# A two-layer attention and MLP kernel whose order comes from a planner: new DMA prices, priorities by stage, and longer runs in a weight load

## The chip, the core and the metric

The kernel runs on one core of a Trainium2 chip. The metric is the device time of one launch in microseconds (us), as the median of several runs. Before the change it was 943.03 us over three runs (942.86 to 943.37).

## What is computed

The input is 2048 tokens of 576 features. Two layers with the same weights follow each other; each is an attention block and an MLP, both with a layer norm ahead and a residual sum behind. Attention has 32 heads of 18 features, and a token sees itself and the 255 tokens before it.

```python
def _A_ref(x, wqkv, wo):            # H = 32, Dh = 18, W = 256
    qkv = (x @ wqkv) ... ; q, k, v = qkv[0], qkv[1], qkv[2]
    scores = jnp.einsum("bhqd,bhkd->bhqk", q, k) * (Dh ** -0.5)
    mask = (idx[:, None] - idx[None, :] >= 0) & (idx[:, None] - idx[None, :] < W)
    p = _softmax(jnp.where(mask[None, None], scores, -1e9), axis=-1)
    return einsum("bhqk,bhkd->bhqd", p, v) ... @ wo

def _B_ref(x, w1, b1, w2, b2):      # w1: 576 x 4608
    h = _gelu(jnp.einsum("bsd,df->bsf", _layernorm(x), w1) + b1)
    return jnp.einsum("bsf,fd->bsd", h, w2) + b2

for _ in range(2):
    x = x + _A_ref(_layernorm(x), A_wqkv, A_wo)
    x = x + _B_ref(x, B_w1, B_b1, B_w2, B_b2)
```

## The kernel before

**Chunks and stages.** The work is cut into eight chunks of 512 tokens, four for each layer. The residual stream (`x_res`) and the attention weights stay in SBUF; the MLP weights w1 and w2 are read from HBM again for each chunk. A chunk k goes through these stages, whose names are those of `PL.stage`:

- `ln`: layer norm of its four 128-token tiles, and a DMA transpose of each into `xnTa` (`ln_norm_T`, issued on L590). The first chunk transposes on TensorE.
- `q<k>.<i>`: q, k and v of tile i (`qkv`, matmuls in `two_out`, L625). VectorE casts them out of PSUM (L647, L660), and q and k are transposed by a DMA (L667).
- `ea`, `eb`: head groups 0 to 3 and 4 to 7 of the attention (`E`). Scores (L695) go to PSUM, ScalarE takes the exponential (L704), GpSimd masks the band's edges (L725), and the product with V (L742) gathers in one PSUM bank. VectorE divides by the sum (L752, L757).
- `t`: the tail (`tail`): four DMA transposes of the attention output into `attT` (L786), the out-projection (L625 again, with `wo_sb`), the residual sum (L776), and the second layer norm with its transpose into `xnTm`.
- `ga`, `gb`: first and second half of the first MLP product with gelu (`G_part`: L820 for the last 64 of 576 rows, L832 for the other 512; gelu on L835).
- `ma`, `mb`: first and second half of the second MLP product (`mm2`, L860) with its residual sum (L776, or L779 into the output tile).

Stages of several chunks are in work at once: while ScalarE is busy with the exponentials of chunk k, TensorE has the MLP products of chunks k-1 and k-2.

**The planner.** The code doesn't issue instructions as it goes; each `add` makes a task with an engine, a cost, a latency and a priority. `Plan.schedule` then simulates the engines by a list: it takes, over all engines, the ready task that can start first, and between equal start times the one with the lowest priority number (L317). The order that comes out is fixed: each engine runs its own list, and waits on semaphores where a task needs another engine's result. A price that is wrong therefore does not break anything; it puts a task too early or too late in its engine's list. `nudge` adds an amount to the priorities of a stage (L204); it is empty before. Up to 140 us of the plan, where TensorE would idle for more than 0.4 us, the planner puts filler matmuls (L533).

**DMA in the plan.** One number, `dma_free`, is the time at which the transfers so far are through (L348, L349). A DMA's latency is the larger of its stated one and what the queue gives plus 1.3 us. A transfer's `move` is its bytes over 270 GB/s (`dma`, L486); transposes state a latency of 2.5 us (4.5 in chunk 0, 4.0 for the attention output) and a move of 0.6. SyncE issues nearly all of them: weight and input loads and transposes stand in one list.

**Weight slots.** `w1_load` (L596) fills one of four slots with a block of 512 columns of w1: one load of 512 KB for the first 512 rows, and two of 32 KB for the other 64 rows. These 64 rows fill only half of the array's rows, so the kernel puts two column tiles on the two halves at once: the two loads go to partitions 0 to 63 and 64 to 127, and `rest` (L814) makes four matmuls in pairs. With `(a b f)` the load for half b takes the tiles b and b+2: two runs of 128 columns, 256 bytes each. `w2_load` (L611) reads w2 in nine pieces of 288 KB for each half.

Of the kernel before, what the change touches and what calls it, by code (L numbers as in the profile page):

```python
# [184 lines left out]
class Plan:  # L185
# [15 lines left out]
        self.fifo_last = {}  # L201

    def add(self, eng, fn, reads=(), writes=(), dma=None, ring=4, cost=0.1, lat=0.1, prio=0.0, alloc=(), fifo=None, plain=False, after=(), move=0.0, hold=False):
        prio += self.nudge.get(self.stage, 0.0)  # L204
        t = Task(idx=len(self.tasks), eng=eng, fn=fn, reads=tuple(reads), writes=tuple(writes), cost=cost, lat=lat, prio=prio,
                 dma=dma, ring=ring, alloc=tuple(alloc), handles=tuple({r for r in tuple(reads) + tuple(writes) if isinstance(r, Bank)}),
                 plain=plain, move=move, fifo=fifo, hold=hold, stage=self.stage)
        pred = set()
        for r in t.reads:
            if r in self.lw:  # L210
                pred.add(self.lw[r])
        for w in t.writes:
            pred.update(self.rd.get(w, ()))
            if w in self.lw:
                pred.add(self.lw[w])
        for w in after:
            pred.update(self.rd.get(w, ()))
        for w in t.writes:
            self.lw[w] = t
            self.rd[w] = []  # L220
        for r in t.reads:
            self.rd.setdefault(r, []).append(t)
        order = set()
        if fifo is not None:
            if fifo in self.fifo_last:
                order.add(self.fifo_last[fifo])
            self.fifo_last[fifo] = t
        order -= pred
        for p in pred:
            p.succ.append((t, True))  # L230
        for p in order:
            p.succ.append((t, False))
        t.npred = len(pred) + len(order)
        for h in t.handles:
            h.left += 1
        self.tasks.append(t)
        return t
# [15 lines left out]
    def schedule(self):  # L253
# [49 lines left out]
        dma_free = 0.0  # L303
        n = len(self.tasks)
        while len(order) < n:
            best = None
            cands = []
            for e in ENGS:
                for t in released[e]:
                    st = max(free[e], t.ready)  # L310
                    got = ()
                    if t.alloc:
                        got, when = place(t)
                        if got is None:
                            continue
                        st = max(st, when)
                    key = (round(st, 3), t.prio, t.idx)  # L317
                    if e == "pe" and st < self.feed_until or t.hold:
                        cands.append((key, t, st, got))
                    if best is None or key < best[0]:  # L320
                        best = (key, t, st, got)
            assert best is not None, "stuck"
            _, t, st, got = best
            if t.eng == "pe" and t.fifo is None and st < self.feed_until and starves(t, st, got):
                for c in sorted(cands, key=lambda c: c[0]):
                    if c[1].fifo is not None or not starves(*c[1:]):
                        _, t, st, got = c
                        break
            if t.eng == "pe" and t.fifo is None:
                for c in cands:  # L330
                    if c[1].hold and c[2] <= st + self.hold:
                        _, t, st, got = c
            if t.eng == "pe" and st < self.warm_until and st - free["pe"] > 0.4:
                self.keep_warm(free["pe"], st, bank_free, extra)
                free["pe"] = st
            released[t.eng].remove(t)
            for h, no in zip(t.alloc, got):
                h.no = no
                for b in h.banks():
                    del bank_free[b]  # L340
            free[t.eng] = st + t.cost
            if t.fifo == "pa":
                fed += 1
                backlog += sum(x.cost for x, data in t.succ if data and x.eng == "act")
            elif t.fifo == "act" and t.handles:
                backlog -= t.cost
            if t.dma is not None:
                dma_free = max(dma_free, st + t.cost) + t.move  # L348
                t.lat = max(t.lat, dma_free + 1.3 - st - t.cost)  # L349
            t.end = st + t.cost + t.lat  # L350
            for h in t.handles:
                h.left -= 1
                h.free = max(h.free, t.end)
                if h.left == 0:
                    for b in h.banks():
                        bank_free[b] = h.free
            for s, data in t.succ:
                same = s.eng == t.eng == "pe"
                s.ready = max(s.ready, st + t.cost + (t.lat if data and not same else 0.0))
                s.npred -= 1  # L360
                if s.npred == 0:
                    released[s.eng].append(s)
            order.append((st, t))
# [16 lines left out]
def build_kernel(nc, A_x, A_wqkv, A_wo, B_x, B_w1, B_b1, B_w2, B_b2, out):  # L380
# [9 lines left out]
    NFH = NF // 2  # L390
# [16 lines left out]
    S = Sched(nc)  # L407
    PL = Plan(S, 7)
    add = PL.add

    def sb(name, shape, dtype):
        return nc.alloc_sbuf_tensor(name, shape, dtype)
# [10 lines left out]
    qn = sb("qn", [P, NQN, H * 32], BF16)  # L423
# [62 lines left out]
    def dma(q, out_, in_, reads=(), writes=(), cls="w", ring=8, **kw):  # L486
        n = 2 if cls != "xr" else 4
        for s in out_.shape:
            n *= s
        add(q, lambda e: e.dma_start(out_, in_), reads=reads, writes=writes, dma=cls, ring=ring, lat=1.3, move=n / 270e3, **kw)  # L490

    n0 = CH[0][2]

# [28 lines left out]
    for i in range(NQN):  # L522
        add("pool", lambda e, i=i: e.memset(qn[:, i, :].rearrange("p (h e) -> p h e", e=32)[:, :, DH:32], 0.0),
            writes=[f"qn{i}h{h}" for h in range(2)], cost=0.5, prio=-9)
# [39 lines left out]
    def ln_norm_T(t, i, dst, dname, prio, src=None, srcres=None, dup=False, pe=False):  # L564
        s = x_res if src is None else src
        res = X(t) if srcres is None else srcres
        sl = xn_ctr[0] % NXN
# [3 lines left out]
            reads=res + [f"mv{t}", f"rstd{t}"], writes=[f"xn{sl}"], cost=0.6, prio=prio)  # L571
# [6 lines left out]
        if pe:  # L578
# [9 lines left out]
                reads=[b], writes=[f"{dname}{i}"], cost=0.75, lat=0.2, prio=prio)  # L588
            return
        add("sp", lambda e: e.dma_start_transpose(dst[:, :, i * 128:(i + 1) * 128], xn[:, sl, :]),  # L590
            reads=rd, writes=[f"{dname}{i}"], dma="t", ring=8, cost=1.3, lat=2.5, move=0.6, prio=prio)


    w1n = [0]

    def w1_load(prio, reads=()):  # L596
        B = w1n[0]
        if B >= NK * 9:
            return
        w1n[0] += 1  # L600
        sl = B % NB1
        bb = B % 9
        cols = slice(bb * 512, (bb + 1) * 512)
        dma("sp", w1_sb[:, sl, 0:2048].rearrange("p (c f) -> p c f", c=4), B_w1[0:512, cols].rearrange("(c p) f -> p c f", p=P),
            reads=reads, writes=[f"w1a{sl}"], cls="w1", cost=0.5, prio=prio)
        src = B_w1[512:576, cols].rearrange("p (a b f) -> p b a f", a=2, b=2)
        for b in range(2):
            dma("sp", w1_sb[64 * b:64 * b + 64, sl, 2048:2304].rearrange("p (a f) -> p a f", a=2), src[:, b],
                writes=[f"w1b{sl}_{b}"], cls="w1", cost=0.5, prio=prio)

    def w2_load(hf, prio, gate=False):  # L611
        for pr in range(NFH // 2):
            f0 = hf * NFH + 2 * pr
            dma("sp", w2_sb[:, 2 * pr:2 * pr + 2, :], B_w2[f0 * P:(f0 + 2) * P, :].rearrange("(w p) d -> p w d", p=P),
                reads=[f"h{2 * pr}"] if gate else [], writes=[f"w2s{pr}"], cls="w2", ring=9, cost=0.6, prio=prio)


    def two_out(lhs, rhs, reads, prio, after=(), fill=FILL):
# [17 lines left out]
    def qkv(k, i, prio0):  # L636
        l, t0, nt = CH[k]
        A = l * NT + t0 + i
        for n, w in enumerate("qkv"):
# [10 lines left out]
            else:  # L650
# [14 lines left out]
                else:  # L665
                    dst, dn = k_of(A)
                add("sp", lambda e, dst=dst, sl=sl: e.dma_start_transpose(dst, qn[:, sl, :]),  # L667
                    reads=[f"qn{sl}h0", f"qn{sl}h1"], writes=[dn], dma="t", ring=8, cost=1.3, lat=2.5 if k else 4.5, move=0.6, prio=prio)


    def units_of(k):
# [110 lines left out]
    def tail(k, prio):  # L782
        l, t0, nt = CH[k]
        rd = [f"aq{g}" for g in range(G)]
        for i in range(nt):
            add("sp", lambda e, i=i: e.dma_start_transpose(attT[:, :, i * 128:(i + 1) * 128], attq[:, i, :]),  # L786
                reads=rd + ["aqd"], writes=[f"aT{i}"], dma="t", ring=8, cost=1.3, lat=4.0, move=0.6, prio=prio - 0.1)
        for i in range(nt):
            t = t0 + i
            bs = two_out(lambda c, i=i: attT[:, c, i * 128:(i + 1) * 128], lambda c, s: wo_sb[:, c, s:s + HB],  # L790
# [8 lines left out]
    def G_part(k, hf, prio):  # L799
# [6 lines left out]
        while f < f1:  # L806
# [7 lines left out]
            def rest(e, fs=fs, sl=sl, bks=bks):  # L814

                ins = None
                for ff, bk in zip(fs, bks):
                    b = ff % 2
                    col = 2048 + (ff % 4) // 2 * 128
                    ins = e.matmul(bank(bk)[:, 0:n], w1_sb[64 * b:64 * b + 64, sl, col:col + 128], xnTm[64 * b:64 * b + 64, k % 2, 4, 0:n],  # L820
                                   start=True, stop=False, tile_position=(64 * b, 0))
                return ins
# [213 lines left out]
```

The softmax here doesn't subtract the row's maximum and nothing guards it: scores larger than these inputs give would overflow.

## Time and profile before

| | |
|---|---|
| time, median of 3 | 943.03 us |
| span of the profiled execution | 942.4 us, mean granted TensorE clock 0.993 |
| MLP products on TensorE, L860 / L832 / L820 | 312.1 / 259.5 / 45.0 us |
| qkv / out-projection, L625 | 134.3 / 43.1 us |
| P times V, L742; scores, L695 | 101.3; 65.1 us (and 12.3 for chunk 1's) |
| filler matmuls, L533 | 12.1 us, 70 of them |
| exponential / gelu on ScalarE | 346.8 / 197.5 us |
| SyncE's and ScalarE's DMA queues | 120.96 and 2.65 MB in 231,248 and 2,432 packets |
| GpSimd's DMA queue | 5.03 MB in 6,880 packets |
| packets under 512 B, of all | 158,768 of 240,663 |
| issue to landing, median: attT, xnTm, kT, qT, xnTa | 3.1, 3.5, 3.3, 3.6, 3.2 us |
| issue to landing, median: w1 512 KB, w1 32 KB, w2 288 KB, x 576 KB | 4.1, 3.8, 4.9, 5.9 us |

Busy times are unions: overlapping matmuls count once. A matmul's mean duration holds its latency, so the count times the mean is more than the busy time. PEld is the weight load ahead of each matmul and overlaps it. The granted clock is given as a share of full speed. A wait is put down to the semaphore that came last.

### The profile page before, as it was taken

How to read it: one execution, taken by the hardware profiler on the slowest of the kernel's cores; microseconds unless marked ns; L12 is line 12 of the kernel's file. 1: busy time of each engine (PE TensorE's matmuls, PEld its weight loads, DVE VectorE, ACT ScalarE, POOL GpSimd, SP SyncE). 2: the span in 40 equal slices, each digit the busy share in tenths (PEclk: the TensorE clock that was granted, in tenths of full speed). 3: DMA queues.
4: the chain of work that ended last, by engine and by line, in shares of the span. 5: the costliest groups of instructions: out<-in, count | busy, mean ns of one | idle time of the engine just before them, and what ended most of it. 6: DMA issues, size and time to landing. Idle time of an engine off the chain costs nothing. (4 is left out here: it accounts for less than half of the span.)

```text
span 942.4 us, 22728 instructions
## 1 busy us (share of the span) xinstructions
PE 906.8 (96%) x9353; PEld 563.4 (60%) x9402; DVE 312.2 (33%) x796; ACT 592.3 (63%) x717; POOL 369.5 (39%) x507
## 2 busy tenths in 40 slices
PE   8798999999999999999999999999999999999998
PEld 6456556564665657655575756647466574746556
DVE  6546312740272303732154321442015320242001
ACT  3687686677827777277833778458783587852541
POOL 3767444373612635135420454316362063620100
PEclk9799999999999999999999999999999999999999
DMA  9997639944295426945159251693709716184440
GB/s 218 149 208 131 171 93 245 185 114 130 60 222 134 137 79 132 172 112 164 51 112 244 60 163 52 142 208 88 216 3 222 163 42 199 30 228 130 149 139 26
DMA packets 240663, 130.10 MB, mean 138 GB/s; under 512 B 158768, under 2 KB 238384, under 8 KB 240560
## 3 DMA queue, kind: packets, MB, share of 16 engines
q1 hardware_dynamic: 231248, 120.96, 54.4%
q0 software_dynamic: 6880, 5.03, 2.9%
q10 hardware_dynamic: 2432, 2.65, 0.9%
q8 instruction: 75, 1.23, 0.5%
q14 instruction: 28, 0.23, 0.1%
HBM read 91.87 MB, written 2.36 MB: 100 GB/s over the span
## 5 line engine op out<-in xcount | busy, mean ns | idle before, releaser
L704 ACT ACTIVATE pT<-ps 128x1024 bf16<-128x1024 f32 (+2 forms) x384 | 346.8, 972 | 92.8 <-PE ps L695 91.5
L725 POOL TENSOR_SCALAR_AFFINE_SELECT pT<-pT 128x512 bf16<-128x512 bf16 (+1 forms) x368 | 279.0, 782 | 261.4 <-ACT pT L704 246.2
L835 ACT ACTIVATE hT<-ps,b1col 128x512 bf16<-128x512 f32 x288 | 197.5, 687 | 224.4 <-PE ps L832 223.3
L860 PE MATMUL ps<-w_sb,hT 128*128 128x288 bf16 x2304 | 312.1, 286 | 2.5 <-DVE x_res L776 1.2
L832 PE MATMUL ps<-xnTm,w_sb 128*128 128x512 bf16 x1103 | 259.5, 379 | 3.4 <-issue 1.1
L860 PEld LDWEIGHTS ps<-w_sb,hT 128*128 128x128 bf16 x2304 | 211.4, 97 | 75.0 <-issue 16.6
L776 DVE TENSOR_TENSOR x_res<-ps,x_res 128x288 f32<-128x288 f32 x160 | 71.2, 450 | 371.7 <-PE ps L860 352.9
L832 PEld LDWEIGHTS ps<-xnTm,w_sb 128*128 128x128 bf16 x1152 | 107.1, 98 | 132.1 <-issue 20.1
L625 PE MATMUL ps<-wqkv,xnTa 128*128 128x288 bf16 x960 | 134.3, 289 | 6.7 <-DVE qn L660 4.5
L742 PEld LDWEIGHTS ps<-vA,pT 128*128 128x128 bf16 x2880 | 92.9, 96 | 33.2 <-issue 14.6
L625 PEld LDWEIGHTS ps<-wqkv,xnTa 128*128 128x128 bf16 x960 | 88.8, 98 | 39.3 <-DVE qn L660 9.1
L742 PE MATMUL ps<-vA,pT 128*128 128x20 bf16 x2880 | 101.3, 172 | 4.4 <-DVE mv_all L548 2.8
L842 POOL TENSOR_TENSOR x_res<-x_res,b2bc 128x576 f32<-128x576 f32 x32 | 44.9, 1402 | 90.6 <-ACT hT L835 90.4
L695 PE MATMUL ps<-qT,kT 32*128 32x384 bf16 (+2 forms) x1216 | 65.1, 280 | 5.4 <-ACT pT L704 4.9
L660 DVE CAST qn<-ps 128x288 bf16<-128x288 f32 x120 | 54.2, 455 | 47.7 <-PE ps L625 47.4
L557 POOL TENSOR_SCALAR vtmp<-mv_all 128x1 f32<-128x1 f32 (+1 forms) x43 | 8.3, 192 | 154.9 <-DVE mv_all L548 154.2
L820 PE MATMUL ps<-xnTm,w_sb 64*128 64x512 bf16 x288 | 45.0, 381 | 2.5 <-ACT pT L704 1.2
L546 DVE BATCH_NORM_STATS2 st_all<-x_res 128x6 f32<-128x288 f32 x104 | 45.2, 449 | 4.8 <-DMA x_res<-in_A_x_dram 3.5
L625 PE MATMUL ps<-wo_sb,attT 128*128 128x288 bf16 x320 | 43.1, 286 | 3.7 <-DMA attT<-attq 3.7
L779 DVE TENSOR_TENSOR xn<-ps,x_res 128x288 bf16<-128x288 f32 x32 | 14.6, 458 | 93.4 <-PE ps L860 93.4
L695 PEld LDWEIGHTS ps<-qT,kT 32*128 32x128 bf16 x1216 | 19.5, 92 | 36.1 <-issue 17.9
L569 DVE TENSOR_SCALAR xn<-x_res,mv_all,rstd 128x576 bf16<-128x576 f32 x52 | 32.9, 636 | 24.6 <-DMA xnTm<-xn 14.9
(39 smaller groups left out, 280.5 us busy)
## 6 DMA issues: line engine op xcount, KB each, us to landing
w_sb<-in_B_w_dram SPq DMA_DIRECT2D x144, 288.0 KB, 4.9
w_sb<-in_B_w_dram SPq DMA_DIRECT2D x72, 512.0 KB, 4.1
w_sb<-in_B_w_dram SPq DMA_DIRECT2D x144, 32.0 KB, 3.8
x_res<-in_A_x_dram POOLq DMA_DIRECT2D x4, 1152.0 KB, 9.0
out_dram<-xn SPq DMA_DIRECT2D x16, 144.0 KB, 1.8
wqkv<-in_A_wqkv_dram ACTq DMA_DIRECT2D x3, 576.0 KB, 7.0
hT<-in_A_x_dram SPq DMA_DIRECT2D x2, 576.0 KB, 5.9
wo_sb<-in_A_wo_dram ACTq DMA_DIRECT2D x1, 576.0 KB, 5.0
```

Of the source, the lines that this page charges most:

```text
L546: add("dve", lambda e, i=i, s=s: e.bn_stats(st_all[:, t, i, :], s[:, t, i * HB:(i + 1) * HB]), reads=res, writes=[f"st{t}_{i}"], cost=0.43 ...
L625: ins = e.matmul(bank(bs[o])[:, 0:HB], lhs(c), rhs(c, o * HB), start=(c == 0), stop=(c == KD - 1))
L660: add("dve", lambda e, b=bs[o], dst=dst: e.tensor_copy(dst, bank(b)[:, 0:HB].rearrange("p (h d) -> p h d", d=DH)), reads=[bs[o]], writes=[ ...
L695: ins = e.matmul(two(bs[j // 2])[:, j % 2, col:col + nq * 128], k_of(T0 + so)[0][32 * j:32 * j + 32, g, :], qs[32 * j:32 * j + 32, g, qo * ...
L704: add("act", lambda e, h2=h2: e.activation(pT[:, sl, 2 * h2:2 * h2 + 2, lo:hi], two(bs[h2])[:, :, lo:hi], ACT.Exp, scale=SCALE), reads=[bs ...
L725: add("pool", lambda e, ap=ap, pat=pat, sgn=sgn, kind=kind: e.affine_select(ap, ap, pattern=pat, compare_op=(ALU.is_ge if kind == "d" else ...
L742: ins = e.matmul(bank(B_O)[:, o:o + VW], pT[:, sl, j, col + qi * 128:col + (qi + 1) * 128], vA[:, (T0 + so) % VS, 4 * g + j, :], start=(fi ...
L776: add("dve", lambda e: e.tensor_tensor(x_res[:, t, sl], bank(b)[:, 0:HB], x_res[:, t, sl], ALU.add), reads=[b], writes=[f"x{t}h{hh}"], cos ...
L820: ins = e.matmul(bank(bk)[:, 0:n], w1_sb[64 * b:64 * b + 64, sl, col:col + 128], xnTm[64 * b:64 * b + 64, k % 2, 4, 0:n], start=True, stop ...
L832: ins = e.matmul(bank(bk)[:, 0:n], w1_sb[:, sl, col:col + 128], xnTm[:, k % 2, c, 0:n], start=False, stop=(c == 3))
L835: add("act", lambda e, ff=ff, fl=fl, bk=bk: e.activation(hT[:, fl, 0:n], bank(bk)[:, 0:n], ACT.Gelu_apprx_tanh, bias=b1col[:, ff:ff + 1]), ...
L860: ins = e.matmul(bank(b)[:, 0:HB], hT[:, fl, i * 128:(i + 1) * 128], w2_sb[:, fl, hh * HB:(hh + 1) * HB], start=(fl == 0), stop=(fl == NFH ...
```

## The change

The planner gets another model of the DMA: each kind of transfer has a stated latency and a service time (`move`), and SyncE's transfers go through one serial queue. `nudge` is filled with amounts for 47 stage names, which were searched for on variations of the planner's own model. Loads of w1, w2 and the residual input get a stage name of their own (with `+`), so that they don't move with the stage that issues them. In the w1 remainder, the load for half b takes the tiles 2b and 2b+1 where all four tiles of the block are used together: one run of 256 columns, 512 bytes. The block that holds the boundary between the two halves of F (tiles 16 and 17 before it, 18 and 19 behind it) stays as it was, and `rest` takes the tiles in the matching order. The computation is the same.

```diff
     def add(...):
-        prio += self.nudge.get(self.stage, 0.0)
+        stage = self.stage + ("+" if dma in ("w1", "w2", "xr") else "")
+        prio += self.nudge.get(stage, 0.0)
 ...
             if t.dma is not None:
-                dma_free = max(dma_free, st + t.cost) + t.move
-                t.lat = max(t.lat, dma_free + 1.3 - st - t.cost)
+                done = max(dma_free, st + t.cost + t.lat) + t.move
+                dma_free = done if t.eng == "sp" else dma_free + t.move
+                t.lat = done - st - t.cost
 ...
+    PL.nudge = {"ld0+": 6.29, "q1.0": -32.21, "q1.2": 2.89, "q1.3": -2.43, "t0": 18.11, "ea1": 3.55, "eb1": 21.57, "ma0": 50.18, "q2.1": 34.5,
+                "q2.3": 41.3, "ea2": -33.88, "ma1+": -2.59, "q3.0": -17.85, "q3.1": -0.47, "q3.2": 6.73, "q3.3": -0.86, "t2": 1.88, "gb1": 14.71,
 ...
+                "ga6": -9.76, "ma6": 4.26}
 ...
-        add(q, lambda e: e.dma_start(out_, in_), reads=reads, writes=writes, dma=cls, ring=ring, lat=1.3, move=n / 270e3, **kw)
+        kw.setdefault("lat", 2.0)
+        kw.setdefault("move", n / 330e3)
+        add(q, lambda e: e.dma_start(out_, in_), reads=reads, writes=writes, dma=cls, ring=ring, **kw)
 ...  ln_norm_T
-            rd, ..., cost=1.3, lat=2.5, move=0.6, prio=prio)
+            rd, ..., cost=1.3, lat=0.6, move=0.8, prio=prio)
 ...  w1_load: large load
-            ..., cls="w1", cost=0.5, prio=prio)
+            ..., cls="w1", cost=0.55, lat=2.0, move=1.45, prio=prio)
         src = B_w1[512:576, cols].rearrange("p (a b f) -> p b a f", a=2, b=2)
+        if not straddles(bb):
+            src = B_w1[512:576, cols].rearrange("p (b a f) -> p b a f", a=2, b=2)
 ...  remainder loads
-                writes=[f"w1b{sl}_{b}"], cls="w1", cost=0.5, prio=prio)
+                writes=[f"w1b{sl}_{b}"], cls="w1", cost=0.6, lat=1.4, move=0.22 if straddles(bb) else 0.15, prio=prio)
 ...  w2_load
-                ..., cls="w2", ring=9, cost=0.6, prio=prio)
+                ..., cls="w2", ring=9, cost=0.55, lat=2.0, move=0.92, prio=prio)
 ...  qkv
-                    ..., cost=1.3, lat=2.5 if k else 4.5, move=0.6, prio=prio)
+                    ..., cost=1.3, lat=0.7, move=1.15, prio=prio)
 ...  tail
-                reads=rd + ["aqd"], ..., cost=1.3, lat=4.0, move=0.6, prio=prio - 0.1)
+                reads=rd + ["aqd"], ..., cost=1.3, lat=0.6, move=0.8, prio=prio - 0.1)
 ...  G_part, rest
-                for ff, bk in zip(fs, bks):
-                    b = ff % 2
-                    col = 2048 + (ff % 4) // 2 * 128
+                at = [(ff % 4, bk) for ff, bk in zip(fs, bks)]
+                if not straddles(fs[0] // 4):
+                    at = [at[i] for i in (0, 2, 1, 3)]
+                for n2, (i, bk) in enumerate(at):
+                    b = n2 % 2
+                    col = 2048 + (i // 2 if straddles(fs[0] // 4) else i % 2) * 128
```

## Prediction

> **What bounds the kernel now.** I read the page first, then the work by stretches of 20 us, then the waits of TensorE, then the timeline around the largest hole. The first two parts of the page say which engine counts:
>
> ```profile
> PE 906.8 (96%) x9353; PEld 563.4 (60%) x9402; DVE 312.2 (33%) x796; ACT 592.3 (63%) x717; POOL 369.5 (39%) x507
> ...
> PE   8798999999999999999999999999999999999998
> ...
> PEclk9799999999999999999999999999999999999999
> ```
>
> TensorE is busy for 906.8 of 942.4 us; 35.6 us are left. Some of those are no idle time: the mlp's first product (L832) has 1103 matmul records and 1152 weight loads, so 49 records are missing, and at about 0.21 us each they explain some 10 us. About 25 us of true idle remain, of which some 4 lie before the first and after the last matmul. The table of stretches shows where:
>
> ```profile
> 0.00:20.00 20.00, 18.16 (x145) 14.30 (x146) 10.86 (x30) 6.70 (x13) 7.39 (x23) 1.00 0.90 220
> 20.00:40.00 20.00, 14.50 (x184) 9.06 (x182) 13.10 (x41) 11.31 (x16) 11.76 (x16) 0.90 1.44 149
> 40.00:60.00 20.00, 17.15 (x219) 10.27 (x216) 10.09 (x22) 13.89 (x20) 13.74 (x20) 0.76 1.01 195
> 60.00:80.00 20.00, 18.89 (x308) 11.98 (x307) 8.07 (x21) 19.14 (x26) 14.95 (x21) 1.00 0.95 178
> 80.00:100.00 20.00, 17.57 (x243) 12.27 (x241) 17.14 (x45) 12.62 (x14) 13.23 (x21) 1.00 0.72 131
> 100.00:943.00 843.00, 820.56 (x8265) 505.53 (x8311) 252.95 (x641) 528.69 (x634) 308.45 (x408) 1.00 0.54 134
> ```
>
> After the window come its length, the busy time of PE, PEld, DVE, ACT and POOL, the granted clock, the DMA share and GB/s. The first 100 us hold 13.7 us of idle TensorE (1.84 + 5.50 + 2.85 + 1.11 + 2.43). In the next 842 us only about 22 are unbusy, of which the missing records take about 10 and the end of the run about 3.5: some 8 us, or 1%. The opening holds two more losses. In the five stretches, 0.90 and 0.76 are a clock at half speed for about 13.7 us; at half speed that costs 6.8 us of matmul time. And the planner's filler matmuls (L533, 12.1 us in all) are idle time that keeps the array running; by stretches, 7.2 us lie before 10 us, where the first inputs are still coming, and 4.9 us between 20 and 80 us.
>
> The timeline of TensorE, and that of VectorE, around the hole that precedes the slow clock:
>
> ```profile
> 32.94 0.93 PE L533 MATMUL ps<-warm 128*128 128x256 bf16 x7
> 33.92 0.29 PE L695 MATMUL ps<-qT,kT 32*128 32x256 bf16 x4
> 36.99 0.47 PE L742 MATMUL ps<-vA,pT 128*128 128x20 bf16 x12 [2.79 <-DVE mv_all L548]
> ...
> 34.77 1.18 DVE L546 BATCH_NORM_STATS2 st_all<-hT 128x6 f32<-128x288 bf16 x3 [3.54 <-DMA hT<-in_A_x_dram]
> ...
> 36.41 0.43 DVE L757 TENSOR_TENSOR attq<-ps,rinv 128x288 bf16<-128x288 f32 x1
> ```
>
> TensorE stands 2.79 us before the probabilities-times-V group. That group needs the mask of POOL, done at about 36.5, and the division on VectorE (L757), done at 36.84; the division stood behind layer norm statistics that waited 3.54 us for an input load. So the load itself holds TensorE up by only some 0.3 us. The rest is that, while exp, mask and division run, nothing else stands next in TensorE's order. That is a matter of order, which this change rewrites.
>
> For the long part, the waits of TensorE alone:
>
> ```profile
> PE ps L695 <- ACT pT L704: 7.1, 16, 1.2
> PE ps L625 <- DVE qn L660: 4.5, 8, 1.4
> PE ps L625 <- DMA attT<-attq: 3.7, 3, 1.4
> PE ps L742 <- DVE mv_all L548: 2.8, 1, 2.8
> ```
>
> The whole list sums to 28 us. No wait on a weight load is in it; the one DMA of weight is the transpose of the attention output before the out-projection, 3.7 us in three of eight chunks.
>
> **The Trainium skill.** "TensorE: Matmul & The Clock Gate", section "What's actually happening", says that the array falls to half clock after an idle window of about 3.4 us and needs a busy one to recover. The trace agrees in kind: clock 1.00 up to 35 us, 0.59 in 35 to 40 and 0.50 in 40 to 45, beginning inside the 2.79 us hole. "DMA: Bandwidth & Descriptors", section "Issuing engines are not separate DMA queues", says that all queues run on the same 16 engines. The trace agrees: while the bias load of POOL took 13.6 us to land, two transposes of SyncE issued between 25 and 45 us took 7.3 us at the median against 3.3 to 3.6 for the q and k transposes of the page. The same page, "Specifications", puts full rate at runs of 512 bytes or more; the packet records show 256-byte packets of about 18 ns and 1024-byte ones of about 46, so a short run does cost more per byte.
>
> **The change part by part.** *Shorter list of packets.* In eight of nine w1 blocks the two remainder loads read 512-byte runs instead of 256-byte ones. There are 144 such loads of 128 runs; 128 of them go to 64 runs, 8,192 packets less. Each pair of 256-byte packets took 36 ns, one of 512 should lie between 18 and 36: at most 8,192 x 18 ns over 16 engines, 9 us of DMA time in all against a DMA share of 0.54. No TensorE wait is for these loads, so I cost it at 0 us, hidden behind the matmuls that run while slots are loaded ahead. The matmuls of `rest` keep number, size and pairing of the row halves; only the order of the banks changes: 0 us.
>
> *DMA prices.* These act only through the order. From issue to landing, old price, new price and trace: attention transposes 5.3, 2.7, 3.1; layer norm transposes 3.8, 2.7, 3.2 and 3.5; q and k transposes 3.8 (5.8 in chunk 0), 3.15, 3.3 and 3.6; large w1 loads 3.7, 4.0, 4.1; w2 pairs 3.0, 3.5, 4.9; the 576 KB input loads 4.1, 4.4, 5.9. (Old: issue cost plus the stated latency, or plus size / 270 plus 1.3. New: cost plus latency plus service.) Loads move towards the trace, and transposes pass from too dear to too cheap by 0.2 to 0.8 us. Too dear meant that the planner put other work before the consumer, which costs nothing while such work is left; too cheap means that the consumer's place in TensorE's fixed order comes early. Behind it every later matmul is held. I take 0.4 us (3.1 - 2.7) as the low end of such a wait and 1.4 us, the longest that the trace shows on this transpose, as the high one, and expect three or four: +1.5 us net.
>
> *Stage priorities.* They add and remove no instruction of the computation; a priority decides only which of the ready tasks of an engine goes first. What can be won is idle time and slow clock. For the opening: the qkv of chunk 1 tile 0 goes far ahead (-32), the tail of chunk 0 and the second half of chunk 1's attention later. That puts ready matmuls into the stretch of 30 to 45 us, where TensorE was busy for 9.58 of 15 us. Bounds: 0 if the hole is only moved; 6.8 (clock) + 2.8 (hole) = 9.6 us if both go. I take the clock and 2.0 of the hole, 8.8 us[...]. For the steady part the bound is the 8 us above; I take half of the attention transposes' wait, 1.9 us, since moving qkv or mlp groups ahead of the out-projection hides it. Sum: -8.8 - 1.9 + 1.5 = -9.2, so 943.0 - 9.2 = 934 us.
>
> **The rivals.** *The hole stays, and the clock drops all the same.* The input load is still priced at 4.4 us, where the one in question took 6.8, and the bias load still has no service time in the plan. For it: both are visible in the lines above. Against: the load was responsible for 0.3 us only. Gain: some waits, 3 to 5 us, so 939. *No difference:* gains in the opening paid back by transposes that land later than planned, 943 +- 1.9. *Slower:* transposes are planned too early at each of eight tails, 8 x 1.4 = 11 us, and less cover ahead of them: 954; with only some tails and a slow clock that lasts as long as now, about 950. For it: the attention transposes took up to 5.0 us where weight loads were in flight, against 2.7 in the plan alone. Against: the new model queues transposes behind loads, so with a busy queue its price rises too.
>
> **How the numbers follow.** 934 in 50 of 100; 939 in 15; no difference in 9; slower in 26. So faster 0.65, same 0.09, slower 0.26. The low end, 921, is the whole of 9.6 plus the 8 us of the steady part and half of the fillers after 20 us and the rest of the opening's holes; the high end, 952, takes in most of the slower case.
>
> **What would show it.** Right: granted clock 1.00 in all stretches of the first 100 us, or a shorter slow one; TensorE's unbusy time there below 10 us; equal instruction counts but for the fillers (70 now); packets under 512 bytes down by about 16,384. Wrong: a slow clock of 13 us or more; waits of L625 on attT above 8 us in total; new waits on xnTm, xnTa or w_sb on TensorE. If TensorE's busy time outside the opening changes by more than 5 us at equal work, the order of its groups costs something that I have taken as nothing.

## Result and the profile after

The changed kernel takes 955.91 us (median of 4, 951.70 to 959.81) against 943.2 us before: a ratio of 1.0134, 95% interval 1.009 to 1.0177. It is slower by 12.7 us. Its four launches spread over 8 us and those of the kernel before over 1, but in later sessions of 15 to 47 launches the latter spread over 5 to 6 us as well.

The page of the kernel after, its first two parts:

```profile
PE 911.4 (96%) x9355; PEld 563.7 (59%) x9396; DVE 316.2 (33%) x796; ACT 592.3 (62%) x717; POOL 368.8 (39%) x507
...
PE   8889999999998999899999999998999899999998
...
PEclk9999999999999999999999999999999999999999
```

The work is the same; the fillers are 64 where they were 70, and 41 matmul records of L854 (L832 before) are missing, where 49 were. TensorE is unbusy for 42.4 us of 953.8, before for 35.6 of 942.4. Less the missing records at about 0.21 us, true idle went from some 25 to some 34 us. Its busy time rose by 4.6 us. The work by stretches, with the columns as before:

```profile
0.00:20.00 20.00, 18.46 (x140) 13.90 (x141) 10.50 (x29) 6.61 (x12) 7.23 (x23) 1.00 0.89 216
20.00:40.00 20.00, 16.23 (x192) 9.40 (x190) 13.28 (x42) 12.08 (x17) 12.51 (x17) 0.91 1.78 154
40.00:60.00 20.00, 16.92 (x249) 10.63 (x246) 11.19 (x26) 14.97 (x22) 14.14 (x21) 1.00 1.14 217
60.00:80.00 20.00, 17.95 (x278) 11.82 (x276) 8.28 (x21) 17.79 (x22) 15.28 (x21) 1.00 0.90 184
80.00:100.00 20.00, 18.18 (x281) 13.31 (x279) 17.45 (x45) 11.76 (x13) 13.38 (x22) 1.00 0.66 102
100.00:954.00 854.00, 823.63 (x8228) 504.60 (x8267) 255.51 (x636) 529.12 (x634) 306.24 (x406) 0.99 0.53 132
```

The opening did what the prediction hoped for, in part: one slow stretch of the clock, of 3.4 us in place of 13.7, and 12.3 us of unbusy TensorE in place of 13.7. All of the loss lies behind it: unbusy time after 100 us went from 21.8 to 30.2 us, and the clock is no longer full there. TensorE's own list of waits shows what came in:

```profile
PE ps L714 <- DMA kT<-qn: 5.4, 2, 4.0
PE ps L644 <- DMA xnTa<-xn: 5.3, 2, 2.8
PE ps L644 <- DVE qn L679: 3.2, 7, 0.8
PE ps L842 <- DMA w_sb<-in_B_w_dram: 3.2, 2, 2.6
...
PE ps L714 <- ACT pT L723: 2.4, 7, 0.8
...
PE ps L644 <- DMA attT<-attq: 2.0, 4, 1.3
...
PE ps L882 <- DMA w_sb<-in_B_w_dram: 1.8, 2, 1.4
```

Before, TensorE waited 3.9 us for transposes and never for a load of w1 or w2; after, the lines put down to the transposes of k, of the layer norm and of the attention output and to the weight loads come to 17.7 us, in a few long waits (1.4 us of it, one wait on k, lies in the opening). The search also won something: the waits on the exponential went from 7.1 to 2.4 us.

The longest of them, on TensorE and then on SyncE's queue (start, duration of the issue):

```profile
753.26 3.63 PE L854 MATMUL ps<-xnTm,w_sb 128*128 128x512 bf16 x16
760.85 0.56 PE L714 MATMUL ps<-qT,kT 32*128 32x384 bf16 x8 [3.96 <-DMA kT<-qn]
...
751.85 0.47 SPq L502 DMA_DIRECT2D w_sb<-in_B_w_dram  x1
752.41 1.23 SPq L602 DMA_TRANSPOSE xnTm<-xn  x1
753.69 2.87 SPq L686 DMA_TRANSPOSE kT<-qn  x1
756.61 1.31 SPq L686 DMA_TRANSPOSE qT<-qn  x1
```

Behind three w2 loads and a transpose, the issue of kT held SyncE for 2.87 us where 1.29 is its median. The line names kT, but kT landed at 759.90 us, 0.95 us before TensorE went on. What ended the hole is the transpose of q behind it: the scores read it, TensorE's own wait on its semaphore lasts from 756.04 to 760.80 us, and it landed at 760.76, 4.2 us after its issue at 756.61. So the held-up issue of kT cost TensorE time by making the next issue late. The same is seen at the holes that end at 295.88 and 404.62 us: there a layer norm transpose and a w1 load landed 2.6 and 3.7 us after their issue, about as usual; their issue was late.

Stretches of half clock follow three of the long holes; after the clock come the DMA share and GB/s:

```profile
290.00:295.00 5.00, 3.10 (x17) 1.47 (x15) 3.49 (x10) 3.85 (x5) 0.93 (x3) 1.00 1.01 225
295.00:300.00 5.00, 4.12 (x26) 2.32 (x27) 3.25 (x7) 1.77 (x2) 0.64 (x1) 0.68 0.77 187
400.00:405.00 5.00, 2.39 (x20) 1.51 (x18) 3.22 (x9) 0.69 (x1) 0.74 (x2) 1.00 0.90 235
405.00:410.00 5.00, 5.00 (x24) 2.68 (x23) 3.37 (x11) 0.25 (x1) 1.48 (x4) 0.66 1.16 266
755.00:760.00 5.00, 1.89 (x9) 0.69 (x7) 0.80 (x2) 3.37 (x5) 0.16 (x1) 1.00 1.28 192
760.00:765.00 5.00, 4.15 (x26) 2.50 (x26) 0.00 (x0) 1.94 (x2) 1.54 (x2) 0.66 1.39 220
```

There are four such stretches of 3.4 us in the steady part, the three shown and one at 539 us; before there was none. At half speed they cost 4 x 1.7 = 6.8 us, so a wait can be paid twice. Not each long hole has one: the one of 2.55 us that ends at 646.58 us has none behind it, and the stretch at 539 us comes with a hole of 0.83 us. With one in the opening that is 8.5 us, against 6.8 us before: the clock alone explains under 2 us of the difference, and more than its gain in the opening was given back.

**The plan against the trace.** The planner knows when it means each group to start, so the n-th weight load of TensorE can be set against the plan. How far TensorE is behind its plan, in us, at five plan times (worked out from the planner's own times and the traces; the experiments are told below):

```
kernel                  plan's end   100    300    500    700    900
before                     939.3     3.0    2.1    2.4    2.3    2.5
after                      926.4     4.2   12.7   17.2   23.7   27.4
model_only                 939.4     4.2    4.2    8.4    8.0    6.9
model_margin1              943.6     0.7    3.1    3.6    2.9    1.8
before_few_bytes           939.3     2.3    1.4    0.6   -1.0   -2.4
after_few_w2               926.4     1.9    6.4    7.7   15.7   14.0
after_few_bytes            926.4     4.5    8.7    9.1   12.3   10.6
after_tfirst               926.4     3.1   11.4   17.4   28.4   32.3
stall_aware                933.7     5.2    7.7    8.4    9.3    9.6
```

The kernel before follows its plan to within 4 us from end to end. The change shortened the plan by 13.0 us, and the chip fell behind that plan by 27 us, by some 3 us in each chunk. In its row hardly anything of a step is won back. The planned idle time of TensorE after the first 100 us is 8.9 us, where it was 17.7 us.

SyncE's issues, set against the plan in the same way, show the difference most plainly. At the tails its list is nearly full in both kernels: the issues that the plan puts between 590 and 620 us took 30.5 us before and 31.3 us after. Before, SyncE fell up to 9.3 us behind its plan (after the first 100 us) and came back to under 1 us, and TensorE stayed between 1.0 and 3.8 us all the while: one attention transpose landed 10.5 us after its issue at 157 us, and TensorE has no wait over 0.7 us between 126 and 187 us. After the change TensorE follows SyncE's steps: between 710 and 740 us of the plan SyncE went from 26 to 31 us behind and TensorE from 23 to 29.

### The profile page after: what moved, and what is told of

The parts are those of the page before. It is cut to its first block, busy times and chain, and to the rows that moved or that the text cites. A ratio compares the mean times of both kernels' runs of the same rounds, so it can differ in the third digit from the quotient of the medians.

```text
span 953.8 us, 22696 instructions
## 1 busy us (share of the span) xinstructions
PE 911.4 (96%) x9355; PEld 563.7 (59%) x9396; DVE 316.2 (33%) x796; ACT 592.3 (62%) x717; POOL 368.8 (39%) x507
## 3 DMA queue, kind: packets, MB, share of 16 engines
q8 instruction: 75, 1.23, 0.6%
## 5 line engine op out<-in xcount | busy, mean ns | idle before, releaser
L882 PE MATMUL ps<-w_sb,hT 128*128 128x288 bf16 x2304 | 317.6, 288 | 4.8 <-DVE x_res L795 2.7
L854 PE MATMUL ps<-xnTm,w_sb 128*128 128x512 bf16 x1111 | 259.5, 380 | 3.7 <-issue 2.1
L854 PEld LDWEIGHTS ps<-xnTm,w_sb 128*128 128x128 bf16 x1152 | 106.8, 98 | 139.7 <-issue 26.2
L644 PE MATMUL ps<-wqkv,xnTa 128*128 128x288 bf16 x960 | 138.8, 291 | 11.0 <-DMA xnTa<-xn 5.3
L761 PEld LDWEIGHTS ps<-vA,pT 128*128 128x128 bf16 x2880 | 94.2, 96 | 23.7 <-issue 10.5
L644 PE MATMUL ps<-wo_sb,attT 128*128 128x288 bf16 x320 | 46.1, 291 | 2.1 <-DMA attT<-attq 2.0
L771 DVE RECIPROCAL rinv<-ps 128x16 f32<-128x16 f32 x64 | 16.4, 256 | 94.3 <-PE ps L761 94.3
```

Of the source, the lines that this page charges most:

```text
L644: ins = e.matmul(bank(bs[o])[:, 0:HB], lhs(c), rhs(c, o * HB), start=(c == 0), stop=(c == KD - 1))
L761: ins = e.matmul(bank(B_O)[:, o:o + VW], pT[:, sl, j, col + qi * 128:col + (qi + 1) * 128], vA[:, (T0 + so) % VS, 4 * g + j, :], start=(fi ...
L854: ins = e.matmul(bank(bk)[:, 0:n], w1_sb[:, sl, col:col + 128], xnTm[:, k % 2, c, 0:n], start=False, stop=(c == 3))
L882: ins = e.matmul(bank(b)[:, 0:HB], hT[:, fl, i * 128:(i + 1) * 128], w2_sb[:, fl, hh * HB:(hh + 1) * HB], start=(fl == 0), stop=(fl == NFH ...
```

## Experiments

Each ratio is to launches of the kernel before in the same session, whose median was 943.6 to 945.2 us. Theory A says that the priorities were fitted to the plan so closely that a late landing is always paid. The rivals: B, the new transpose prices are too low in themselves; C, the 512-byte runs; D, the new order costs TensorE time by itself; E, the priorities leave ready transposes standing behind weight loads.

### The parts of the change one by one

**Prices and runs without priorities**

```diff
-    PL.nudge = {"ld0+": 6.29, ...}
+    PL.nudge = {}
```

> The changed kernel with an empty table of stage priorities: the new DMA prices and the 512-byte runs alone. The plan's own end is 939.4 us (before 939.3, changed 926.4). Theory A (the searched priorities leave nothing between a planned landing and its use, so each late landing holds TensorE, and the lateness adds up): without them the time is near that of before, 942 to 949 us. Theory B (the new prices of the transposes are too low, whatever the priorities; the step that my prediction's slower rival names): 950 us or more. Theory C (the runs of 512 bytes): 950 us or more too.

Measured: 946.74 us, ratio 1.0012 (1.0001 to 1.0024). The new prices change the order and almost nothing of the time, so B is not the cause. By the two ratios, 1.0134 and 1.0012, the table of priorities on these prices costs 11.5 us. TensorE's waits on the attention transposes grew a little, 5.1 us in four where it was 3.7 in three:

```profile
PE ps L709 <- ACT pT L718: 8.2, 18, 1.2
PE ps L639 <- DMA attT<-attq: 5.1, 4, 2.9
```

**Priorities without the prices**

```diff
 # the kernel before, with
+    PL.nudge = {"ld0+": 6.29, ...}      # and the "+" on the stage names of w1, w2, xr
```

> The kernel before with the table of stage priorities (and the split of the stage names) but its own DMA prices and runs. The plan's own end is 955.7 us. Theory A: priorities that were searched for on one set of prices have no worth on another, 953 to 965 us. If the priorities are good in themselves and the new prices are the fault (theory B), it is at or below 943 us.

Measured: 981.81 us, ratio 1.0391 (1.0353 to 1.0429), worse than expected. The mean clock was 0.974. On other prices the table is worth less than no table: the plan itself loses 16 us, the chip 37. So the table's worth in the plan doesn't carry over to this second set of prices; no other was tried.

**The runs alone**

```diff
-        src = ...rearrange("p (a b f) -> p b a f", a=2, b=2)
+        src = ...rearrange("p (b a f) -> p b a f", a=2, b=2)   # but for the straddling block; and the order in rest
```

> The kernel before with the 512-byte runs in the w1 remainder loads and the matching matmul order alone; order and prices as before, plan's own end 939.3 us. Theory A (the searched priorities): same as before within 0.2%. Theory C (the runs cost time): 948 us or more.

Measured: 944.79 us, ratio 1.0003 (0.999 to 1.0016). C falls. The packets went down by 8,192 in all and by 16,384 under 512 bytes, as worked out in the prediction, and TensorE waited for no weight load.

### The same order with less traffic

**All weight loads small**

```diff
+        mo, mi = part or (out_, in_)      # from each buffer's second fill on: one run of 128 bytes in a row
-        add(q, lambda e: e.dma_start(out_, in_), ...)
+        add(q, lambda e: e.dma_start(mo, mi), ...)
```

> The changed kernel with the same order on every engine, but after the first fill of each buffer the loads of w1 and w2 move 128 (or 64) rows of 128 bytes instead of the whole block, so most weights are stale and the result is not the reference's; the plan still prices the whole. Theory A, with late landings as the cause: the waits on transposes and weights go, and the time falls to 928 to 936 us (the plan's 926.4 and the 3 us of the opening). A rival D (the new order costs TensorE time by itself, by more switches between groups of matmuls): it stays at 948 us or more.

> The kernel before with its order and the same small weight loads; most weights are stale and the result is not the reference's. Theory A: the order of before had spare time ahead of its transposes, so it gains only its waits on the attention transposes and a part of the opening, 937 to 942 us, and the changed order with small loads is faster than this one. Rival D: as fast as before or faster, and faster than the changed order with small loads.

Measured: the changed order 939.89 us, ratio to before 0.9937 (0.9918 to 0.9955); the order of before 940.4 us, 0.994 (0.9918 to 0.9962). By the ratios (1.0134 with the whole loads) weight traffic costs the order of before some 6 us and the changed order some 19. The difference, 13 us, is the whole of the loss, so D falls as the reason for it. But the expectation of theory A was missed too: without the traffic the two orders are equal, and the 13 us by which the plan of the changed one is shorter do not appear. At 900 us it is still 10.6 us behind its plan, while the order of before is 2.4 us ahead of its own. TensorE waits 4.3 us for layer norm transposes even then. So how much of the planned gain this order could give without the traffic is open, and D as a reason for that gap is not excluded.

**Only w2 small**

> The changed kernel, same order, with only the loads of w2 small after the first fill (w1 whole); most w2 weights are stale and the result is not the reference's. With all weight loads small the changed kernel took 939.9 us. If the w2 loads that stand ahead of transposes in SyncE's list are most of the delay: 942 to 947 us. If w1 is: 950 us or more.

Measured: 942.0 us, 0.9978 (0.9965 to 0.9991): about 15 of the 19 us come from w2, whose loads stand among the transposes of a tail, as in the lines at 752 us above.

```profile
PE ps L650 <- DMA xnTa<-xn: 4.2, 2, 3.3
PE ps L888 <- DVE x_res L801: 3.6, 8, 1.4
PE ps L650 <- DVE qn L685: 3.2, 7, 0.8
...
PE ps L720 <- DMA kT<-qn: 1.7, 2, 1.1
```

The waits put down to kT fell from 5.4 to 1.7 us and those on weight loads from 5.0 to 1.1; one wait of 3.3 us on a layer norm transpose is left.

**The same bytes in fewer descriptors**

```diff
-   B_w2[f0 * P:(f0 + 2) * P, :].rearrange("(w p) d -> p w d", p=P)
+   B_w2[f0 * P:(f0 + 2) * P, :].rearrange("(p w) d -> p w d", p=P)
```

> The changed kernel, same order and same bytes, but each w2 load gives a partition two neighbouring rows of w2, so that it moves 128 runs of 2304 bytes instead of 256 of 1152 (w2's rows then stand in another order than the product needs, so the result is not the reference's). If the number of descriptors that w2 loads put ahead of transposes is what holds SyncE and the landings up: 942 to 950 us, most of the 14 us that small w2 loads gave. If it is the bytes, that is the time of service: 951 to 957 us as before the edit.

> The kernel before with the same edit of the w2 loads (same restriction on its result). Descriptors: 0 to 3 us faster than before, as with small loads (5 us). Bytes: the same within 0.2%.

Measured: 952.68 us, 1.0078 (1.0052 to 1.0104), and 944.26 us, 0.9997 (0.9985 to 1.0009). The first is where the bytes were expected to leave it; by the ratios it is 5 us faster than the changed kernel, but the two intervals overlap, so a gain is not shown. Small w2 loads gave 15. Small loads and this edit both leave 128 packets in a load, so they differ by the bytes, and the difference of 9 us (1.0078 against 0.9978) is clear of the noise. The packet records show that the edit also shortened the service a little: one 2304-byte packet takes 93 ns, two of 1152 take 102. So the time for which w2's bytes occupy the queue is the larger part; how much the count of descriptors adds by holding SyncE is not settled by this. In single traces the transposes whose issue took over 2 us, after the first 100 us, go the same way: 9 in the changed kernel and 9 with this edit, 5 with small w2 loads, 2 with all weight loads small.

### Does it help to let transposes go first?

```diff
+        # after planning, SyncE's list alone: a transpose whose inputs are ready moves ahead of
+        # the weight loads, and of transposes that became ready later, in front of it
```

In the plan of the changed kernel two transposes of stage q7 are ready at 706.7 us and are issued at 725.7 and 727.0, behind w1 and w2 loads and other transposes; the table adds 2.21 and 9.48 to their priorities and nothing to those of these loads. That made theory E plausible.

> The changed kernel with one edit to SyncE's list alone: after planning, each DMA transpose whose inputs the plan has ready moves ahead of the weight loads (and of transposes that became ready later) in front of it. All other engines keep their lists, and all DMAs are the same. Longest planned stand of a ready transpose: 20.3 us before the edit, 7.0 after it. Theory E (what hurts is that the priorities leave ready transposes behind weight loads): 941 to 948 us. Theory A (the searched order has no time to spare anywhere, and any DMA that comes late by SyncE's held-up issue is paid): 951 to 958 us, since the same descriptors are out at the same times.

> The kernel before with the same edit to SyncE's list. Longest planned stand of a ready transpose: 10.8 us before the edit, 5.6 after it. Theory E: up to 3 us faster, by its waits on the attention transposes. Theory A: the same within 0.3%, since these transposes had time to spare.

Measured: 959.69 us, ratio 1.0163 (1.0117 to 1.0209), and 945.86 us, 1.0015 (0.9999 to 1.003). The remedy that E suggests does not help. What it was aimed at went down: the waits on xnTa from 5.3 to 1.6 us, those put down to kT from 5.4 to 3.7 and those on weight loads from 5.0 to 3.4. The attention transposes, 2.0 us in the changed kernel, took their place, as TensorE's list shows:

```profile
PE ps L668 <- DMA attT<-attq: 9.5, 5, 4.2
PE ps L668 <- DVE qn L703: 4.1, 7, 1.1
PE ps L738 <- DMA kT<-qn: 3.7, 3, 1.4
...
PE ps L668 <- DMA xnTa<-xn: 1.6, 2, 0.9
```

In SyncE's queue five q and k transposes and four weight loads now stand directly in front of the attention transposes of one tail. The first of these is issued at 745.89 us; its product starts at 751.67, after a hole of 4.16 us. So putting transposes ahead of loads is no cure while SyncE's list is full; that loads in front of ready transposes cost nothing is not shown.

### Spare time in the plan

**Each landing 1 us later in the plan, no priorities**

```diff
-                t.lat = done - st - t.cost
+                t.lat = done - st - t.cost + 1.0
```

> The changed kernel with an empty table of priorities, and 1.0 us added in the plan to every DMA's landing but not to its service: spare time ahead of each use. The plan's own end is 943.6 us (939.4 without the spare time). Theory A: the time follows the plan more closely than with the new prices alone, 942 to 946 us, and the waits of TensorE on transposes are below 3 us (7 us with the prices alone). Theory B says no different from the prices alone, or slower by the plan's 4 us: 948 to 951 us.

Measured: 946.42 us, 1.0023 (1.0009 to 1.0037). The plan's end and the chip now agree to 2 us at the end, but the time is no better than with the prices alone, since the plan itself got 4 us longer. TensorE still waited 3.4 us for the attention transposes and 1.4 for kT, more than expected. Here spare time made the plan come true; it didn't make it short.

**A search against a less kind model**

```diff
-    PL.nudge = {"ld0+": 6.29, ...}                  # searched for the plan's end
+    PL.nudge = {... 103 stage names ...}            # searched for the played-through end
-                t.lat = done - st - t.cost
+                t.lat = done - st - t.cost + 0.9
```

> The changed kernel's DMA prices and 512-byte runs, with two edits: 0.9 us of spare time is added in the plan to every DMA's landing, and the stage priorities come from a search of the same kind whose aim is not the plan's end but the end of the fixed order when it is played through with SyncE's issue held up while many descriptors are out, and with landings 0.3 to 0.8 us late. (The second half of a final output tile also takes a proper write order.) The plan's own end is 933.7 us, 7 us later than that of the changed kernel; played through with held-up issue it ends at 939 us, against 955 for the changed kernel and 950 for before. Theory A with held-up issue as the cause: the time is 930 to 938 us, faster than both kernels, and the lag of TensorE behind its plan stays below 8 us. If searched priorities do not hold on the chip whatever they are searched on (theory D, the order's own cost): 943 us or more.

Measured: 945.57 us, 1.0026 (1.001 to 1.0043). It is about 10 us faster than the changed kernel with a plan that ends 7 us later, so a shorter plan is not a better one. Whether the other aim of the search or the spare time did it is not shown, since both were changed at once. And the expectation was missed: it is slower than before by a quarter of a percent, and 9.6 us behind its plan at 900 us. The played-through model had put it 11 us ahead of before, 939 against 950 us; it was 6 to 7 us too low for the one and as much too high for the other. No version that was run with whole weight loads beat the kernel before clear of the noise.

## Why the prediction was wrong

**Direction and size.** 934 us was forecast, with 0.65 for faster; 955.91 is beyond the high end of 952. The case that came true was the slower rival, at 954 us, which had 26 of 100; since its sum was of other waits, its closeness to 955.91 is luck.

**What held.** The 512-byte runs cost nothing (1.0003) and the counts of packets came out as worked out. The opening's step had the right sign: the slow clock shrank from 13.7 to 3.4 us, which is 5.1 of the 6.8 us at stake. The hole was not closed so much as spread: unbusy time in the first 100 us fell by 1.5 us where 2.0 was put on one hole. The 1.9 us put on the attention transposes nearly came too: TensorE's waits on them went from 3.7 to 2.0 us. And of the signs of being wrong, the new waits on xnTa and w_sb were seen.

**The step that failed.** "too cheap means that the consumer's place in TensorE's fixed order comes early ... expect three or four: +1.5 us net". The mechanism was named there and its size was wrong by a factor of about ten. Behind the opening TensorE's unbusy time rose by 8.4 us, some 10 with the missing records counted alike, and four stretches of slow clock added 6.8. Two things were left out of the term. First, I compared prices with landings transfer by transfer and found them 0.2 to 0.8 us too low. On that measure the new prices are good: with them alone the time is the same (1.0012), and in the changed kernel the layer norm transposes into xnTa land 2.7 us after their issue at the median, exactly their price, while two waits on them still cost 5.3 us. What this fixed order paid for is not the mean error of a price but each single transfer that came late, in at least three of the four holes over 2.5 us because its issue in SyncE's list was late. Second, the search was an addition to the change that I costed as "decides only which of the ready tasks of an engine goes first", with 0 as its worst outcome in the opening and a gain in the steady part. On the new prices that term measured +11.5 us on the chip (1.0134 against 1.0012) beside -13 in the plan. That a search on a model picks just those orders which profit where the model is too kind would explain it, and goes with the nudge_only run; it is not shown apart.

**The rival's own reason** was half right. Waits on late transposes were a part of the cause, but hardly at the tails' attention transposes, 2.0 us where 11 was put; the transposes of q and k, the layer norm's and the weight loads took the rest. The figure given for it, "up to 5.0 us where weight loads were in flight", is the median of four transposes; the longest took 10.5 us, and TensorE did not wait for it. And the argument against it, that "the new model queues transposes behind loads, so with a busy queue its price rises too", did not protect: in the example at 753 us the plan had kT behind the same loads, but it gave its issue 1.3 us where it took 2.87, and SyncE's whole list behind it moved, the q transpose that TensorE waited for first.

**The Trainium skill's part.** "TensorE: Matmul & The Clock Gate", section "What's actually happening", gives an idle window of about 3.4 us. The prediction used it for the opening alone. The run shows a hole of 3.96 us, but also holes of 2.8 and 2.6 us, each followed by 3.4 us of half clock, and one of 2.55 us that was not. The 2.79 us hole before the change was shorter than the page's window too. So shorter holes sufficed here, and the length alone does not decide. I should have put a price on every new wait of some length, and not only counted the clock as a gain.

**What stays open.** Why the changed order, with all weight loads small, is still 10.6 us behind its plan: late layer norm transposes are seen, not explained. And what holds SyncE's issue, for up to 3.7 us in the changed kernel: it is rarer with fewer bytes out and was not rarer with fewer descriptors at equal bytes, but these are counts of single traces. The small loads also shortened SyncE's issues as a whole, from 430.5 to 401.7 us, and how much of their gain comes by that and how much by faster landings is not separated.

## What to carry to other kernels

A fixed order that was searched for on a model is worth what it yields when single transfers come late, so set the trace against the plan step by step, for the engine that issues the DMAs too, and don't count a shorter plan as a gain before that. A price that is too dear is spare time in the plan: with the new prices alone TensorE was 6.9 us behind its plan at 900 us, where it had been 2.5, and 1 us more on each landing brought it back to 1.8. By itself that hardly moved the time; under a searched order the same lateness was paid. When TensorE is busy for 96%, a wait of 3 us costs its own length and may cost about half again in slow clock.

## What the runs showed of the hardware

- The issue of a DMA transpose takes SyncE 1.23 to 1.31 us at the median; 19 of 156 took more than 2 us before the change, 13 after it, up to 4.4 and 3.7 us. So the held-up issues were there before, and by the lags above the order of before had time for them.
- A packet of 256 bytes took 18 ns at the median, of 512 bytes 27, of 1152 51, of 2304 93 (each on its DMA engine). The Trainium skill's "DMA: Bandwidth & Descriptors", section "Specifications", puts full rate at 512 bytes or more; here the cost per byte still falls from 512 to 2304 bytes, by 23%.
- A stretch of half clock lasted 3.4 us or a multiple of it, 13.7 at most, in all of these traces but for the last microseconds of a run.
